# Two attentions in one kernel: A's value projection moved behind B's query and key projections, and the row maxima 52 steps ahead instead of 24

## The chip, the cores and the metric

The kernel runs on 1 core of one Trainium2 chip. A core has a matrix engine (TensorE, PE in the profile, with PEld for its weight loads), a vector engine (VectorE, DVE), an engine for activations (ScalarE, ACT), a general one (GpSimd, POOL), a queue that issues the DMAs here (SyncE, SP), and 16 DMA engines. Each engine runs its own instructions in program order. PE writes only to the accumulator memory of 8 banks (`ps_st`), from which ACT and DVE read.

The metric is the device time of one execution in microseconds (us), lower is better. Before the change it is 1758.52 us, the median of 3 runs (1756.85 to 1760.27).

## What is computed

Two attentions over the same shapes (sequence S = 2048, D = 640, 32 heads of 20 columns), each with its own x, weights and output projection; the two outputs stand side by side.

```python
def _A_ref(x, wqkv, wo):                    # sliding window: 8 keys, 2 apart
    qkv = (x @ wqkv) -> q, k, v             # (1, 32, 2048, 20) each
    idx = pos[:, None] - (arange(8) * 2)    # negative positions are masked
    logits = einsum("bhsd,bhswd->bhsw", q, k[idx]) * 20 ** -0.5
    o = einsum("bhsw,bhswd->bhsd", softmax(logits), v[idx])
    return o @ wo
def _B_ref(x, wqkv, wo):                    # full attention
    p = softmax(einsum("bhqd,bhkd->bhqk", q, k) * 20 ** -0.5)
    return einsum("bhqk,bhkd->bhqd", p, v) @ wo
return concatenate([a, b], axis=-1)
```

## The kernel before

**Precision.** Every operand x or W of a projection is split in two parts, hi and lo (`split`: a copy, then a subtraction), and a product is three passes (`PASSES`): hi·hi, hi·lo, lo·hi. With the contraction of 640 cut into `KC` = 5 chunks of 128, one output tile of a projection is 15 matmuls.

**Stage 1, projections.** First A's 1920 columns q, k, v, in `NA` = 4 column groups (`A_COLS`: 512, 384, 512 and 512 wide), each for 16 row tiles of 128 positions: 15 matmuls per tile, then a copy by ACT (`a_store`) and a store to memory. Then B's q and k, transposed: 40 groups of 15 matmuls 512 wide (the loop over `m`, `n`, `j`). Then B's v: 32 groups (`v_group`) of one row tile and half of the columns (320). From the seventh group on such a group runs in row halves: 30 matmuls with a contraction of 64, in two banks at once, which POOL adds (`ve<-ve,more`). x of A and B (`xn`, `xl`) lies in four big buffers; when B's v is computed, two of its four chunks have been overwritten by the first heads' q and k (`bq`, `bk`) and are loaded again.

**Stage 2, the loop over B's attention.** The heads go in 8 stacks of 4 (`NG`, `GH`); for each stack there are 4 blocks of queries (`NQC`) and 16 blocks of keys (`NKB`), `NS` = 512 steps in all. A step has for PE: 4 matmuls for scores (`b_qk`/`s_matmul`, contraction 62 rows, in the trace `ps_st<-bq,bk 62*128`), 4 for the row maxima of a step that comes later (`m_matmul`, 60 rows, `ps_st<-bk,bq 60*128`), and the 4 products with v (`b_pv`, `ps_st<-e,vb`; 8 records in the trace). DVE reduces the maxima (`mx<-ps_st`, 512 elements or, where two banks lie side by side, 1024 at once), ACT does the exponentials (`e<-ps_st`, 4 per step) and copies the products out (`more`), POOL adds these to `braw`. The maxima of 16 steps together make one unit; at its end (`max_rows`) they are turned by DVE, split by POOL, sent through memory (`mdr`) and enter the score matmuls as two more rows of `bq`.

The maxima of step i + `LEAD` are computed at step i. The first `LEAD` = 24 are computed ahead of the loop, one after each of the v groups (`b_max`), and in the last `LEAD` steps there are none. The order of the loop's matmuls is a string, `ORDER`: V starts a step, S is two score matmuls, M two maxima, Y one of each, N two single maxima, H a piece of A's output projection, and the digits are the banks.

**A's attention** runs on POOL beside all this: 128 units (`UNITS`), 64 of scores (`akv<-akv,aq` and a tree of additions) and 64 of values (`akv<-akv,al`, `ao`), four of each for a tile of 128 positions. Each unit's k or v rows (`akv`) are loaded two units ahead. In the loop a unit's pieces are handed out by an estimate of POOL's time, `STEP` = 2.47 us per step. In stage 1 a unit is handed out at some of B's q and k groups (`a_unit`).

## Time and profile before

The profiled execution took 1756.04 us; from its first to its last instruction (the span) it is 1754.3 us.

| what | us | from |
|---|---|---|
| time, median of 3 | 1758.52 | runs |
| time of the profiled execution | 1756.04 | its run |
| span of the profiled execution | 1754.3 | page, first line |
| busy PE / DVE / ACT / POOL | 1736.7 / 1335.1 / 1341.2 / 1253.5 | page, part 1 |
| A's projections, from the first full run of matmuls | 8.2 to 211.7 | PE's timeline |
| B's q and k | 211.7 to 348.5 | PE's timeline |
| B's v, with 24 maxima | 348.5 to 428.5 | PE's timeline |
| the 488 steps that have maxima | 428.5 to 1639.4 | PE's timeline |
| the last steps and the end of B's output projection | 1639.4 to 1754.3 | PE's timeline |

How to read it: a group of instructions is named out<-in by the tiles it writes and reads. Two numbers go with it, the time in which at least one of the group ran (busy), and the mean duration of one; where instructions of an engine overlap, the count times the mean is more than the busy time. Matmuls are pipelined, and their ends are modelled, so the distance from one start to the next says more of PE than the busy share. PEclk is the clock granted to PE, 1.00 being full.

### The profile page before, as it was taken

How to read it: one execution, taken by the hardware profiler on the slowest of the kernel's cores; microseconds unless marked ns; L12 is line 12 of the kernel's file. 1: busy time of each engine (PE TensorE's matmuls, PEld its weight loads, DVE VectorE, ACT ScalarE, POOL GpSimd, SP SyncE). 2: the span in 40 equal slices, each digit the busy share in tenths (PEclk: the TensorE clock that was granted, in tenths of full speed). 3: DMA queues.
4: the chain of work that ended last, by engine and by line, in shares of the span. 5: the costliest groups of instructions: out<-in, count | busy, mean ns of one | idle time of the engine just before them, and what ended most of it. 6: DMA issues, size and time to landing. Idle time of an engine off the chain costs nothing.

```text
span 1754.3 us, 33331 instructions
## 1 busy us (share of the span) xinstructions
PE 1736.7 (99%) x12051; PEld 1000.7 (57%) x12051; DVE 1335.1 (76%) x1792; ACT 1341.2 (76%) x2649; POOL 1253.5 (71%) x1128
## 2 busy tenths in 40 slices
PE   9999999999999999999999999999999999999999
PEld 8988888898335444444445444443444444453569
DVE  3100232368999999999999999999999989999300
ACT  4222322233999999999999999999999989999981
POOL 0000058335899999999999999999999998447242
PEclk9999999999999999999999999999999999999999
DMA  6323597763644444364435336344444534122123
GB/s 232 113 97 107 175 307 251 263 190 114 193 128 130 128 134 141 109 170 130 139 110 163 117 105 174 117 153 124 142 128 126 142 117 118 33 60 77 33 71 116
DMA packets 191197, 240.32 MB, mean 137 GB/s; under 512 B 89020, under 2 KB 115260, under 8 KB 190040
## 3 DMA queue, kind: packets, MB, share of 16 engines
q1 hardware_dynamic: 190456, 237.54, 44.4%
q8 instruction: 94, 1.54, 0.4%
q14 instruction: 71, 0.58, 0.1%
q10 hardware_dynamic: 576, 0.66, 0.1%
HBM read 173.21 MB, written 64.91 MB: 136 GB/s over the span
## 4 chain that ended last, share of the span: by engine, by line
PE 70%; POOL 11%; DVE 10%; DMA 5%; issue 2%; ACT 1%; SPq 1%; POOLq 0%; DVEq 0%; ACTq 0%
PE ps_st L66 70%; DVE mx L66 10%; POOL akv L66 6%; POOL braw L66 3%; ACT e L66 1%; SPq L66 1%; DMA bq<-qb_d 1%; DMA stg<-wo_a 1%; DMA bk<-kb_d 1%; DMA akv<-va_d 1%; POOL ao L66 1%; POOL aot L66 1%; POOL ww L66 0%; POOL al L66 0%; DMA vb_d<-ve 0%
## 5 line engine op out<-in xcount | busy, mean ns | idle before, releaser
L66 DVE TENSOR_REDUCE mx<-ps_st 128x1 f32<-128x512 f32 (+1 forms) x1470 | 1214.8, 891 | 29.4 <-PE ps_st L66 25.6
L66 ACT ACTIVATE e<-ps_st 128x512 f32<-128x512 f32 x2048 | 1069.2, 618 | 56.9 <-PE ps_st L66 38.6
L66 PE MATMUL ps_st<-bq,bk 62*128 62x512 f32 x2048 | 563.3, 437 | 7.8 <-DMA bq<-mdr 3.6
L66 PE MATMUL ps_st<-bk,bq 60*128 60x512 f32 x2048 | 551.3, 437 | 4.1 <-DVE mx L66 2.4
L66 PE MATMUL ps_st<-e,vb 128*32 128x512 f32 x4096 | 544.0, 605 | 0.7 <-ACT e L66 0.2
L66 PEld LDWEIGHTS ps_st<-bq,bk 62*128 62x128 f32 x2048 | 282.3, 184 | 416.7 <-ACT e L66 267.6
L66 POOL TENSOR_TENSOR akv<-akv,aq 128x1280 f32<-128x1280 f32 x64 | 189.0, 2953 | 234.0 <-DMA akv<-ka_d 234.0
L66 POOL TENSOR_TENSOR braw<-braw,more 128x512 f32<-128x512 f32 x224 | 288.1, 1286 | 68.2 <-ACT more L66 67.7
L66 PEld LDWEIGHTS ps_st<-bk,bq 60*128 60x128 f32 x2048 | 257.8, 184 | 108.5 <-DVE mx L66 54.0
L66 POOL TENSOR_TENSOR akv<-akv 128x640 f32<-128x640 f32 (+3 forms) x304 | 282.4, 929 | 14.3
L66 ACT COPY ro<-ps_st 128x320 f32<-128x320 f32 (+2 forms) x156 | 72.2, 491 | 175.4 <-PE ps_st L66 125.8
L66 PEld LDWEIGHTS ps_st<-e,vb 128*32 128x32 f32 x4096 | 82.2, 108 | 152.1 <-issue 75.8
L66 POOL TENSOR_TENSOR akv<-akv,al 128x1280 f32<-128x1280 f32 x64 | 152.1, 2377 | 0.2
L66 ACT COPY more<-ps_st 128x512 f32<-128x512 f32 (+1 forms) x248 | 144.7, 584 | 3.9 <-PE ps_st L66 2.4
L66 PE MATMUL ps_st<-wc,xn 128*128 128x512 f32 (+1 forms) x576 | 133.5, 376 | 0.0
L66 PE MATMUL ps_st<-ww,xn 64*128 64x320 f32 (+1 forms) x1056 | 125.1, 310 | 0.2 <-ACT ve L66 0.2
L66 PEld LDWEIGHTS ps_st<-ww,xn 64*128 64x128 f32 (+1 forms) x1056 | 116.0, 186 | 13.7 <-ACT e L66 7.1
L66 PEld LDWEIGHTS ps_st<-wc,xn 128*128 128x128 f32 x576 | 106.2, 188 | 17.9 <-ACT xn L66 0.4
L66 PE MATMUL ps_st<-xn,w 128*128 128x512 f32 x480 | 115.8, 390 | 0.0
L66 PEld LDWEIGHTS ps_st<-xn,w 128*128 128x128 f32 x480 | 90.1, 188 | 19.4
L66 ACT CAST pr<-ps_st 128x512 fp32r<-128x512 f32 x40 | 23.5, 587 | 101.5 <-PE ps_st L66 98.7
L66 PE MATMUL ps_st<-ww,aot 64*128 64x320 f32 x960 | 99.4, 308 | 0.0
(66 smaller groups left out, 1011.2 us busy)
## 6 DMA issues: line engine op xcount, KB each, us to landing
akv<-ka_d SPq DMA_DIRECT2D x128, 320.0 KB
akv<-va_d SPq DMA_DIRECT2D x128, 320.0 KB
kb_d<-pr SPq DMA_DIRECT2D x20, 512.0 KB
qb_d<-pr SPq DMA_DIRECT2D x20, 512.0 KB
bk<-kb_d SPq DMA_DIRECT2D x16, 640.0 KB
bq<-qb_d SPq DMA_DIRECT2D x64, 160.0 KB
rb<-s_d SPq DMA_DIRECT2D x128, 64.0 KB
stg<-xb SPq DMA_DIRECT2D x12, 512.0 KB
```

The costliest lines, as they stand in the source:

```text
L66: return self.tc.keep_in_program_order(op(*a, **k))
```

## The change

1. A's projections before B's are q and k only: `A_COLS` has three groups of 512, 256 and 512 columns.
2. A's v is computed after B's q and k, as B's v is: A's 32 groups of 320 columns, then B's 32. For this x of A is loaded and split a second time, chunk by chunk, and then x of B (`x_load`; the lo part by POOL for 7 of the 8 chunks, before for 2).
3. Of these 64 groups 52 run in row halves, but in another way: two groups at once, group one on the upper rows of the array and group two on the lower ones, then the other way round, so that each adds up in one bank. POOL's additions `ve<-ve,more` are gone. The first 4 groups, and 8 at the end (two of them inside the loop, as before), run plain.
4. `LEAD` is 52: after each of the 52 groups in row halves stands one `b_max`. The loop keeps its 488 steps with an `ORDER` (`TAIL` = 24 steps follow), but has 460 steps' maxima in them. `ORDER` is a new string.
5. A's units: the scores run 3 tiles ahead of the values (`R_AHEAD`), the values wait until A's v rows are there (`v_rows`), and units are handed out by POOL's estimated time in stage 1 too (`a_pace`). `STEP` is 2.4. A unit of values is not begun while two finished tiles wait to be turned.
6. The loads of the next stack's q and k start at step 1 of a stack, not 4, and the first eight go two per step.

```diff
-LEAD = 24
+LEAD = 52
+TAIL = 24
+R_AHEAD = 3
-STEP = 2.47
+STEP = 2.4
+QK_US = 3.42
+V_US = 2.72
-    A_COLS = [0, 512, 896, 1408, 3 * D]
+    A_COLS = [0, 512, 768, 2 * D]
...
+    UNITS = [(t, c) for k in range(NT + R_AHEAD) for t, cs in ((k - R_AHEAD, range(4, WIN)), (k, range(4))) if 0 <= t < NT for c in cs]
...
+            while any(u[1] >= 4 and v_rows[0] <= u[0] for u in UNITS[n:n + 3]) or c == 4 and len(done_a) > 1:
+                yield False
...
+    def a_pace(us):
+        gp.us = max(gp.us, us - 2.5)
+        while gp.us < us + AHEAD and next(a_work, 0) is not False:
+            if not a_work.gi_frame:
+                break
...
-                if 4 < groups < 34 and groups * 2 % 5 < 2:
-                    a_unit()
+                if groups > 4:
+                    a_pace(QK_US * groups)
...
+    def v_matmuls(c, half, s, p, r=None, start=True, stop=True):
+        rows = slice(0, 128) if r is None else slice(r * HALF, r * HALF + HALF)
+        for k in range(KC):
+            for i, (wi, xi) in enumerate(PASSES):
+                yield pe.matmul(p[:, :320], chunk(XV[c][0], xi, k)[rows, s % 4 * 128:s % 4 * 128 + 128], WV[c // 4][half][wi][rows, k],
+                                start=start and k == 0 and i == 0, stop=stop and k == KC - 1 and i == 2)
...
+    def v_tick(us, maxima=True):
+        for i in islice(steps, int(maxima)):
+            b_max(i)
+        tick()
...
+        v_us[0] += us
+        a_pace(v_us[0])
+    def x_load(c, w):
+        x, pieces = x_pieces((xa, xb)[c // 4], c % 4, gp)
+        XV.append((x, pieces))
+        wait[0] = w
+        for fn in pieces:
+            fn()
...
+    x_load(1, 5)
+    for block in range(15):
+        c, half = divmod(block, 2)
+        s0 = c % 4 * 4
+        if block in (0, 14):
+            for s in range(s0, s0 + 4):
+                v_group(c, half, s)
+                v_tick(2.2, False)
+        else:
+            ps4 = [bank() for _ in range(4)]
+            for second in range(2):
+                for u in range(2):
+                    for _ in zip(*(v_matmuls(c, half, s0 + 2 * u + (r ^ second), ps4[2 * u + (r ^ second)], r, second == 0, second == 1) for r in range(2))):
+                        pass
...
+                    v_tick(V_US)
+        if half:
+            if c < 6:
+                x_load(c + 2, 3)
+            if c < 4:
+                after(2, v_rows.__setitem__, 0, 4 * c + 4)
...
-        if sub == 4 and g + 1 < NG:
-            k_loads, q_loads = b_pieces(g + 1)
+        if sub == (1 if g else 2) and g + 1 < NG:
+            k_loads, q_loads = b_pieces(g + 1) if g else ([], q1_loads)
...
-                after(1 + 2 * n, fn)
+                after(1 + (n // 2 if n < 8 else 2 * n - 12), fn)
```

Where this moves instructions is shown at three places. The first is PE's program in A's projections, at the seam between the first and the second column group (`wc` and `wd` are the chunks 0 to 2 and 3 to 4 of the weight, `xn` and `xl` those of x). Before:

```order
L66 MATMUL ps_st<-wc,xn 128x512 x9
L66 MATMUL ps_st<-wd,xn 128x512 x3
L66 MATMUL ps_st<-wd,xl 128x512 x3
L66 MATMUL ps_st<-wc,xn 128x384 x9
L66 MATMUL ps_st<-wd,xn 128x384 x3
L66 MATMUL ps_st<-wd,xl 128x384 x3
```

After:

```order
L70 MATMUL ps_st<-wc,xn 128x512 x9
L70 MATMUL ps_st<-wd,xn 128x512 x3
L70 MATMUL ps_st<-wd,xl 128x512 x3
L70 MATMUL ps_st<-wc,xn 128x256 x9
L70 MATMUL ps_st<-wd,xn 128x256 x3
L70 MATMUL ps_st<-wd,xl 128x256 x3
```

The second group's 240 matmuls are 256 wide in place of 384, and one of the three groups of 512 (another 240 matmuls) is gone from this stage.

The second place is DVE's program from the end of B's q and k to the first steps of the loop (`ww` is a half of the weights of v being split, `mx` the maxima, `128x2` a reduction of 1024 elements, `128x1` one of 512; `mtr` is the turn at a unit's end). Before:

```order
L66 TENSOR_REDUCE mx4_2648<-ps_st_66 128x2 x32
L66 TENSOR_REDUCE mx1_2486<-mx4_2648 128x16
L66 STREAM_TRANSPOSE mtr_3298<-mx1_2486 128x32
L66 TENSOR_REDUCE mx4_3339<-ps_st_66 128x2 x16
L66 TENSOR_REDUCE mx4_3339<-ps_st_66 128x1
L66 TENSOR_REDUCE mx4_3339<-ps_st_66 128x2 x2
```

After, the first unit and the beginning of the second:

```order
L70 TENSOR_REDUCE mx4_2292<-ps_st_66 128x2 x12
L70 RECIPROCAL am_1543<-am_1543 128x32
L70 TENSOR_REDUCE mx4_2292<-ps_st_66 128x2 x16
L70 TENSOR_REDUCE am_2865<-al_1696 128x32
L70 TENSOR_REDUCE mx4_2292<-ps_st_66 128x2 x4
L70 TENSOR_REDUCE mx1_2156<-mx4_2292 128x16
L70 STREAM_TRANSPOSE mtr_2956<-mx1_2156 128x32
L70 TENSOR_REDUCE mx4_2994<-ps_st_66 128x2 x4
```

Before, 48 reductions of 1024 elements (24 steps) stand ahead of the loop's first single one; after the change 104 do (52 steps), with pieces of A's softmax (`am`, `al`) between them.

The third place is POOL's program in the groups of v (`ve<-ve,more` adds the row halves, `xn<-stg,xn` and `xl<-stg,xl` make the lo part of a chunk of x, `akv` and `al` are A's units). Before:

```order
L66 TENSOR_TENSOR ve<-ve,more 128x16x20 x7
L66 TENSOR_TENSOR xn<-stg,xn 128x1024 x2
L66 TENSOR_TENSOR xl<-stg,xl 128x512
L66 TENSOR_TENSOR ve<-ve,more 128x16x20 x8
L66 TENSOR_TENSOR xn<-stg,xn 128x1024 x2
```

After:

```order
L70 TENSOR_TENSOR xn<-stg,xn 128x1024 x2
L70 TENSOR_TENSOR xl<-stg,xl 128x512
L70 TENSOR_TENSOR al<-al,am 128x256
L70 TENSOR_TENSOR akv<-akv,aq 128x1280
L70 TENSOR_TENSOR akv<-akv 128x2x320
L70 TENSOR_TENSOR xn<-stg,xn 128x1024 x2
L70 TENSOR_TENSOR xl<-stg,xl 128x512
L70 TENSOR_TENSOR akv<-akv 128x2x160
```

The additions of the halves are gone, and the lo parts of x, which PE needs for the next groups, now stand in one line with A's units.

More of the change, by code (lines that the diff above doesn't have):

```diff
@@ L867, in attention_pair, with b_row @@
     steps = iter(range(LEAD))
[L868 to L871 removed]
+    WV = [[w0, w1], [None, None]]
+    def b_row(half, s, p):
         ve = ones[s % 4]
         to = ve[:, :16 * VC].rearrange("p (h c) -> p h c", c=VC)[:, :, :DH]
[L874 to L892 removed]
@@ L895, in attention_pair, with a_row @@
-    V_GROUPS = [(n, half, s) for n in (2, 3, 0, 1) for half in range(2) for s in range(4 * n, 4 * n + 4)]
-    v_late = V_GROUPS[-LAG:]
-    for n, half, s in V_GROUPS[:-LAG]:
-        v_group(n, half, s, groups > 5)
+        act.copy(to, p[:, :320].rearrange("p (h d) -> p h d", d=DH))
+        give(p)
+        c = 16 * VC + 11 * half
+        after(1, sp.dma_start, vb_d[s * 128:(s + 1) * 128, half * 16 * VC:half * 16 * VC + c], ve[:, :c])
+    def a_row(half, s, p):
+        hf, r0 = divmod(s * 128, HS)
+        store_rows(p, va_d[hf, PAD + r0:PAD + r0 + 128, half * 320:half * 320 + 320])
@@ new lines, in v_matmuls, with v_group @@
+    def v_matmuls(c, half, s, p, r=None, start=True, stop=True):
[4 more added lines that the diff above has]
+                                start=start and k == 0 and i == 0, stop=stop and k == KC - 1 and i == 2)
+    def v_group(c, half, s):
+        p = bank()
+        for _ in v_matmuls(c, half, s, p):
+            pass
+        (b_row if c > 3 else a_row)(half, s, p)
@@ L951, in begin @@
             run_jobs(soft_jobs, 1)
[L952 removed]
+        if done_a and done_a[0][0] <= 0 and len(turned) + len(turn_jobs) < 2:
             a_turn(*done_a.pop(0)[1:])
@@ L956, in begin @@
         while i >= A_FROM and gp.us < i * STEP + AHEAD:
-            if next(a_work, 0) == 0:
+            if next(a_work, 0) is False:
+                break
+            if not a_work.gi_frame:
                 for d in done_a:
@@ L1058, in attention_pair @@
     loop[1] = False
-    for i in range(NS - LEAD, NS + LAG):
+    for i in range(NS - TAIL, NS + LAG):
         begin(i)
```

219 lines of the change are left out of this document (99 added, 120 removed).

## The prediction

> **What bounds the kernel now.** I read the page first, then the busy time per stage, then per stage what DVE, ACT and PE wait for. The page:
>
> ```profile
> span 1754.3 us, 33331 instructions
> PE 1736.7 (99%) x12051; PEld 1000.7 (57%) x12051; DVE 1335.1 (76%) x1792; ACT 1341.2 (76%) x2649; POOL 1253.5 (71%) x1128
> ```
>
> PE's 99% is a share of modelled ends and hides what it waits for, so I cut the span where PE's timeline changes its work. The columns are the stretch, its length, then busy PE, PEld, DVE, ACT, POOL, the granted clock and the DMA share.
>
> ```profile
> 8.20:211.70 203.50, 203.49 (x949) 174.78 (x949) 31.83 (x43) 59.98 (x106) 0.00 (x0) 1.00 0.43 141
> 211.70:348.50 136.80, 136.80 (x602) 112.61 (x601) 45.02 (x59) 35.25 (x58) 79.19 (x68) 1.00 0.79 269
> 348.50:428.50 80.00, 79.26 (x903) 74.72 (x903) 57.15 (x52) 26.74 (x62) 30.82 (x31) 1.00 0.52 163
> 428.50:1639.40 1210.90, 1198.84 (x8794) 547.97 (x8792) 1194.25 (x1626) 1147.74 (x2281) 1105.40 (x982) 1.00 0.43 124
> 1639.40:1754.30 114.90, 111.45 (x782) 84.63 (x780) 4.76 (x10) 67.80 (x140) 34.65 (x33) 1.00 0.26 83
> ```
>
> The first three stretches are PE's: nothing else is busy for more than 0.72 of them. The fourth, the 488 steps with maxima, is DVE's: busy 1194.25 of 1210.9 us, 98.6%, where ACT has 94.8% and POOL 91.3%. Of what is DVE's time made, and what does it wait for there (428.5 to 1639.4)?
>
> ```profile
> L66 DVE TENSOR_REDUCE mx<-ps_st 128x1 f32<-128x512 f32 (+1 forms) x1425 | 1161.9, 881 | 11.8 <-PE ps_st L66 8.0
> L66 DVE TENSOR_REDUCE am<-al 128x32 f32<-128x256 f32 x14 | 8.6, 614 | 3.6 <-POOL al L66 3.6
> ```
>
> 1161.9 us are the maxima themselves. Is it really DVE and not POOL, which is as full until about 1500 us (the last of the busy times in the first pair of rows)? The exponentials (4 per step, in the second pair of rows) count the steps with POOL full and with POOL half idle:
>
> ```profile
> 428.50:1500.00 1071.50, 1060.46 (x7776) 485.33 (x7776) 1055.79 (x1435) 1014.17 (x2016) 1034.06 (x912) 1.00 0.46 134
> 1500.00:1639.40 139.40, 138.38 (x1022) 62.64 (x1024) 138.46 (x192) 133.57 (x266) 71.34 (x70) 1.00 0.19 53
> ```
>
> ```profile
> 450.00:1420.00 970.00, 420.95 (x3160) 62.29 (x3160) 825.32 (x1579) 1.00 0.46 135
> 1500.00:1620.00 120.00, 52.13 (x392) 7.64 (x392) 101.86 (x196) 1.00 0.22 61
> ```
>
> 970 / (1579 / 4) = 2.457 us per step, then 120 / (196 / 4) = 2.449. POOL's relief gives nothing, so A's units on POOL are covered now, and moving them is worth something only through what they delay.
>
> **The change part by part.**
>
> *A's projections.* PE's rows for one row tile, by the distance of the starts:
>
> ```profile
> 86.53 1.72 PE L66 MATMUL ps_st<-wc,xn 128*128 128x384 f32 x9
> ...
> 89.13 1.72 PE L66 MATMUL ps_st<-wc,xn 128*128 128x384 f32 x9
> ...
> 204.82 2.21 PE L66 MATMUL ps_st<-wc,xn 128*128 128x512 f32 x9
> ...
> 208.26 2.21 PE L66 MATMUL ps_st<-wc,xn 128*128 128x512 f32 x9
> ...
> 350.70 1.91 PE L66 MATMUL ps_st<-ww,xn 128*128 128x320 f32 x12
> ...
> 352.89 1.92 PE L66 MATMUL ps_st<-ww,xn 128*128 128x320 f32 x12
> ```
>
> 15 matmuls take 3.44 us at 512 columns, 2.60 at 384, 2.19 at 320. One group of 512 goes: 16 x 3.44 = 55.0 us. The group of 384 becomes one of 256, which the trace does not have. The three rows lie on a line (0.84 us per 128 columns), which gives 1.76 at 256, and a gain of 16 x 0.84 = 13.4; if weight loads set a floor at the 320 row, it is 16 x (2.60 - 2.19) = 6.6. I take the line, since 320 still lies on it. Sum: -68.4 (or -61.6). The weight loads of this stage:
>
> ```profile
> L66 PEld LDWEIGHTS ps_st<-wc,xn 128*128 128x128 f32 x576 | 106.2, 188 | 17.9 <-ACT xn L66 0.4
> ```
>
> They last 188 ns each, more than the line's 1.76 / 15 = 0.117 us per matmul, but overlap each other, so the row settles nothing. The Trainium skill ("TensorE: Matmul & The Clock Gate", LDWEIGHTS) puts a load of 128 columns at about 107 ns whatever the contraction, which would set no floor above the line: by the page -68.4, by the longer loads of the row -61.6. B's q and k, 136.8 us, do not change.
>
> *The groups of v.* Now 62 groups before the loop in place of 30. What one in row halves with its maximum costs:
>
> ```profile
> 417.72 0.69 PE L66 MATMUL ps_st<-bk,bq 60*128 60x512 f32 x4
> ...
> 423.64 1.92 PE L66 MATMUL ps_st<-ww,xn 64*128 64x320 f32 x24
> 425.40 0.60 PE L66 MATMUL ps_st<-ww,xl 64*128 64x320 f32 x6
> 425.84 0.63 PE L66 MATMUL ps_st<-bk,bq 60*128 60x512 f32 x4
> ...
> 428.52 0.68 PE L66 MATMUL ps_st<-bk,bq 60*128 60x512 f32 x4
> ```
>
> ```profile
> L66 DVE TENSOR_REDUCE mx<-ps_st 128x2 f32<-128x1024 f32 x578 | 696.9, 1215 | 20.6 <-PE ps_st L66 19.3
> ```
>
> Four periods in 10.80 us, 2.70 each, of which 2.20 (423.64 to 425.84) are the group: halves cost PE what a plain group does. Two groups together are 60 such matmuls where before they were two times 30, so I take the same. 52 x 2.70 + 10 x 2.19 = 162.3 us, against 80.0: **+82.3**. DVE has two reductions of 1.2 us per period (below) and is covered. POOL's additions of the halves go (hidden, worth 0).
>
> *The first maximum* comes sooner and needs q from memory:
>
> ```profile
> 348.50 1.93 PE L66 MATMUL ps_st<-ww,xn 128*128 128x320 f32 x12
> ...
> 352.57 2.87 SPq L66 DMA_DIRECT2D bq<-qb_d  x4
> ...
> 365.25 0.73 PE L66 MATMUL ps_st<-bk,bq 60*128 60x512 f32 x3 [0.54 <-DMA bq<-qb_d]
> ```
>
> The load was issued 4.1 us into the stage and had landed 16.7 us into it. After the change PE gets there after 4 plain groups and one half pair, 4 x 2.19 + 2.2 = 11.0 us. It waits up to 5.7 us; behind it in PE's queue stand all further groups, so the wait is paid in full. I take **+5**.
>
> So the loop starts -68.4 + 82.3 + 5 = **+18.9 us later**. The second load of x is 8 chunks; its issues on SP stand between the groups, its lo parts on POOL:
>
> ```profile
> L66 POOL TENSOR_TENSOR xn<-stg,xn 128x1024 fp32r<-128x1024 f32 x4 | 9.6, 2408 | 0.3
> L66 POOL TENSOR_TENSOR xl<-stg,xl 128x512 fp32r<-128x512 f32 x2 | 2.6, 1292 | 0.0
> ```
>
> One chunk is 2 x 2.41 + 1.29 = 6.1 us of POOL, handed over three groups after its load and needed five groups (13.5 us) later: hidden if POOL is less than 7.4 us behind. I count 0, its price is below.
>
> *The loop.* 28 of 488 steps' maxima leave it, 28 x 4 = 112 reductions of 512 elements. The window above holds 533 wide and 892 single ones, 1958 halves in 1161.9 us, 0.593 us each: -66.5 us of DVE. Wide reductions become a smaller share (454 of the loop, with 932 single), which gives some 4 us back. DVE's busy time falls from 1194.3 to about 1132 us. What is late next is ACT, 1147.7 us, whose work does not change. Before, the loop was 1210.9 / 1194.3 = 1.014 times its fullest engine's busy time. The same 1.4% over ACT gives 1164; over DVE, 1148, since ACT's busy time counts the overlap of exponentials with gaps between them. I take **1160 us**, 2.38 per step, nearer to ACT's. That is -50.9.
>
> Two more edits act on waits only: the scores running three tiles ahead and the larger lead give A's softmax and the turned maxima more time. The trace has one such wait of size, the 3.6 us of `am` on POOL above (it reached PE):
>
> ```profile
> 1432.13 0.79 PE L66 MATMUL ps_st<-bq,bk 62*128 62x512 f32 x1 [3.14 <-DVE mx L66]
> ...
> 1430.00:1438.00 8.00, 5.87 (x24) 2.68 (x24) 5.67 (x8) 3.12 (x6) 7.76 (x8) 0.61 0.55 179
> ```
>
> The wait was followed by a stretch with the clock at 0.61. Some 8 us hang on it; I leave them inside the 1.4%, since new waits can take its place. The Trainium skill ("TensorE: Matmul & The Clock Gate", Part 1) says that PE idle for a window of about 3.4 us gets half its clock until it was busy for as long. By that rule, with which the trace agrees here (0.61 after 3.14 us of idling), the 5 us wait at the first maximum would cost 2 to 3 us more, and the sum be some 3 us higher.
>
> The earlier loads of the next stack and the end (114.9 us, PE's) I count at 0: the next stack's q and k are hidden behind steps in either case.
>
> *Sum:* 1756.04 + 18.9 - 50.9 = 1724.0 for an execution like the profiled one. That one lies 2.5 us below the median of the runs shown, so I forecast 1726.5, rounded **1727**.
>
> **The rivals.**
>
> 1. *The step is set by the round of banks, not by DVE.* PE fills a bank, ACT empties it, PE may fill it again. For it:
>
> ```profile
> L66 PEld LDWEIGHTS ps_st<-bq,bk 62*128 62x128 f32 x2048 | 282.3, 184 | 416.7 <-ACT e L66 267.6
> ```
>
> The score matmuls' weight loads wait for ACT most of all. Against it: DVE is idle for 11.8 us before its maxima, ACT for 63 in all (1210.9 - 1147.7). If the steps stay near 2.45, fewer maxima bring nothing and the loop takes 1205: 1756 + 18.9 - 6 + 2.5 = 1771, slower. It decides from a loop above 1192 us, 2.44 per step, on. Chance 0.13.
>
> 2. *Lo parts of x late on POOL.* If POOL runs over 7.4 us behind in the groups of v, PE stands before each of 7 chunks, up to 6.1 us, 43 in all. At half of that 1748. Chance 0.08.
>
> 3. *DVE stays the limit,* ACT's overlap being free. Then 1.4% over 1132, less the 8 us around the clock's fall, about 1137: 1704. Chance 0.14.
>
> 4. *A near tie.* DVE and ACT within 2% of each other, POOL close behind: each one's short waits no longer fall into another's, and the loop takes 1180 to 1192. 1747 to 1759. Chance 0.13.
>
> That the change does not do what it says (the maxima leave the loop) is excluded by the order of the instructions.
>
> **How the numbers follow.** My forecast (loop 1148 to 1175) has 0.52. The range goes from 1698 (below rival 3, with the clock's fall gone) to 1762 (all of rivals 2 and 4), leaving out most of rival 1 and tails, together about 0.18. Faster by over 0.2%, below 1755 (about what a measurement of this kernel can tell): 0.52 + 0.14 + 0.10 of rival 4 + 0.05 of rival 2 = 0.81. Within 0.2%: 0.05. Slower: 0.14.
>
> **What would show it.** The end of A's projections near 143 us (150 if a floor exists); 2.70 us from maximum to maximum in the groups of v; PE's wait for `bq<-qb_d` before the first; the loop's start near 447; DVE in the loop near 97%, ACT near 99%; 84 exponentials per 50 us where there were 81. Wrong it would be by long PE waits for POOL `xn`, or by fewer than 82 exponentials per 50 us in the loop with DVE at 93%.

## The result, and the profile after

The changed kernel takes 1779.54 us (median of 4 runs, 1776.89 to 1781.89) against 1759.02 for the kernel before (4 runs): ratio 1.0118, 95% interval 1.0099 to 1.0136. It is slower by 1.2%; the forecast was 1727, the range ended at 1762. The page of the profiled execution (1781.89 us):

```profile
span 1780.1 us, 34705 instructions
PE 1734.6 (97%) x12711; PEld 1014.8 (57%) x12711; DVE 1358.2 (76%) x1814; ACT 1340.4 (75%) x2658; POOL 1265.4 (71%) x1119
```

PE has as much work as before in a longer span. Cut at the same places as in the prediction, with the same columns (stretch, length, busy PE, PEld, DVE, ACT, POOL, clock, DMA share):

```profile
5.20:143.90 138.70, 138.65 (x724) 118.83 (x722) 28.46 (x38) 46.94 (x84) 0.00 (x0) 1.00 0.51 164
143.90:283.20 139.30, 137.38 (x602) 112.46 (x601) 48.70 (x59) 37.96 (x61) 69.05 (x67) 1.00 0.76 259
283.20:471.60 188.40, 170.54 (x1919) 159.78 (x1917) 137.50 (x129) 47.53 (x96) 142.70 (x111) 0.95 0.64 208
471.60:1665.40 1193.80, 1173.04 (x8677) 535.55 (x8678) 1138.09 (x1579) 1138.09 (x2277) 1015.55 (x895) 0.99 0.41 117
1665.40:1780.10 114.70, 111.17 (x780) 84.38 (x778) 4.55 (x10) 67.39 (x139) 34.65 (x33) 1.00 0.27 84
```

| stretch | forecast, us | measured, us | off by |
|---|---|---|---|
| A's projections, up to | 143.3 | 143.9 | +0.6 |
| B's q and k | 136.8 | 139.3 | +2.5 |
| groups of v | 162.3 + 5 | 188.4 | +21.1 |
| the 488 steps with maxima | 1160 | 1193.8 | +33.8 |
| the rest | 114.9 | 114.7 | -0.2 |

The first and the last are right. In B's q and k PE stands 1.9 us in two waits for DVE's split of the weights (`w`), which are most of the 2.5 us there; why they are there was not looked into. In the groups of v PE is idle for 17.9 us, and the clock is at 0.95. Two waits make most of it. PE's timeline at the first:

```profile
306.98 0.76 PE L70 MATMUL ps_st<-bk,bq 60*128 60x512 f32 x1 [11.00 <-DMA bq<-qb_d]
```

SP's timeline, and the clock and the DMA share (the last three columns are clock, share, GB/s) around it:

```profile
289.73 2.22 SPq L70 DMA_DIRECT2D stg<-xa  x3
293.08 0.34 SPq L70 DMA_DIRECT2D va_d<-ro  x1
293.90 7.97 SPq L70 DMA_DIRECT2D bq<-qb_d  x4
```

```profile
271.00:283.00 12.00, 12.00 (x54) 9.81 (x54) 5.08 (x7) 5.48 (x9) 0.00 (x0) 1.00 0.98 308
283.00:295.00 12.00, 11.18 (x82) 10.34 (x82) 4.51 (x7) 4.32 (x9) 0.00 (x0) 1.00 0.94 267
295.00:307.00 12.00, 1.00 (x15) 0.77 (x11) 0.03 (x1) 2.71 (x3) 3.10 (x2) 0.65 0.73 215
```

The load of bq is issued 10.7 us into the stage (4.1 before), four issues take 8 us (2.9 before), and the DMA engines have been nearly full since 271. Around the same seam of the kernel before they were at 0.79 and 0.84:

```profile
336.00:348.00 12.00, 12.00 (x54) 9.85 (x53) 4.27 (x7) 3.37 (x6) 0.00 (x0) 1.00 0.79 255
348.00:360.00 12.00, 12.00 (x82) 11.88 (x81) 2.75 (x4) 4.01 (x8) 0.00 (x0) 1.00 0.84 265
```

The second wait, on PE, on DVE and on POOL:

```profile
387.41 0.79 PE L70 MATMUL ps_st<-bk,bq 60*128 60x512 f32 x2 [4.32 <-DVE mx L70]
```

```profile
380.24 5.98 DVE L70 TENSOR_TENSOR ww<-stg,ww 128x640 fp32r<-128x640 f32 x3
386.14 4.61 DVE L70 TENSOR_REDUCE mx<-ps_st 128x2 f32<-128x1024 f32 x4
...
398.98 1.95 DVE L70 TENSOR_TENSOR ww<-stg,ww 128x640 fp32r<-128x640 f32 x3
```

```profile
379.41 2.98 POOL L70 TENSOR_TENSOR akv<-akv,aq 128x1280 f32<-128x1280 f32 x1
382.47 4.45 POOL L70 TENSOR_TENSOR akv<-akv 128x640 f32<-128x640 f32 x4
```

The same three lo parts of a weight (first half of wv_b, then the second) take DVE 5.98 us while POOL works, and 1.95 us where POOL stands. The maxima queue behind them.

In the loop DVE and ACT are now equal (95.3% of the stretch each). DVE's longest waits there, in total, times and longest:

```profile
DVE mx L70 <- PE ps_st L70: 30.9, 64, 6.6
DVE turn L70 <- POOL ww L70: 8.9, 1, 8.9
DVE sm L70 <- DMA sm<-s_d: 4.7, 2, 3.9
DVE am L70 <- POOL al L70: 3.9, 1, 3.9
```

### The profile page after: what moved, and what is told of

Read it like the earlier page. It is cut to its first block, busy times and chain, and to the rows that moved or that the text cites. A ratio compares the mean times of both kernels' runs of the same rounds, so it can differ in the third digit from the quotient of the medians.

```text
span 1780.1 us, 34705 instructions
## 1 busy us (share of the span) xinstructions
PE 1734.6 (97%) x12711; PEld 1014.8 (57%) x12711; DVE 1358.2 (76%) x1814; ACT 1340.4 (75%) x2658; POOL 1265.4 (71%) x1119
## 5 line engine op out<-in xcount | busy, mean ns | idle before, releaser
L70 PE MATMUL ps_st<-bk,bq 60*128 60x512 f32 x2048 | 563.4, 439 | 31.1 <-DVE mx L70 19.2
L70 PE MATMUL ps_st<-bq,bk 62*128 62x512 f32 x2048 | 549.9, 433 | 0.9 <-ACT e L70 0.6
L70 PEld LDWEIGHTS ps_st<-bq,bk 62*128 62x128 f32 x2048 | 274.6, 185 | 407.8 <-ACT e L70 260.1
L70 PE MATMUL ps_st<-ww,xn 64*128 64x320 f32 (+1 forms) x1776 | 189.9, 313 | 0.8 <-DVE ww L70 0.6
L70 PEld LDWEIGHTS ps_st<-ww,xn 64*128 64x128 f32 (+1 forms) x1776 | 178.3, 190 | 16.3 <-ACT e L70 8.3
L70 ACT COPY more<-ps_st 128x512 f32<-128x512 f32 x224 | 135.7, 606 | 5.3 <-PE ps_st L70 4.6
L70 POOL TENSOR_TENSOR xn<-stg,xn 128x512 fp32r<-128x512 f32 (+1 forms) x30 | 53.8, 1805 | 81.8 <-ACT xn L70 80.5
L70 PEld LDWEIGHTS ps_st<-ww,aot 64*128 64x128 f32 x960 | 91.7, 186 | 4.9 <-issue 0.7
```

The lines of the kernel that those rows point to most:

```text
L70: return self.tc.keep_in_program_order(op(*a, **k))
```

## The experiments

From here the loop is measured from the start of the first score product to the start of the last product for a maximum, both on PE, which is 3.2 us less than the prediction's stretch before the change and 2.7 less after: 1207.7 us before, 1191.1 after, forecast 1157. The places are those of one profiled execution each; the medians are of 4 to 12 runs, and the kernel before took 1757 to 1759 us on each chip.

| kernel | median, us | ratio to before | first maximum | loop starts | loop, us |
|---|---|---|---|---|---|
| before | 1759.0 | | 364.2 | 429.0 | 1207.7 |
| changed | 1779.5 | 1.0118 (1.0099 to 1.0136) | 307.0 | 471.6 | 1191.1 |
| q_first | 1778.8 | 1.0116 (1.0098 to 1.0134) | 305.0 | 469.4 | 1190.0 |
| no_x1 | 1774.5 | 1.0096 (1.0083 to 1.0110) | 301.7 | 465.9 | 1190.4 |
| q_no_x1 | 1775.3 | 1.0089 (1.0076 to 1.0103) | 301.9 | 465.7 | 1190.6 |
| early | 1772.6 | 1.0083 (1.0070 to 1.0095) | 301.1 | 463.1 | 1188.0 |
| lo_pool | 1837.2 | 1.0443 (1.0423 to 1.0463) | 306.1 | 463.8 | 1248.9 |
| lo_same | 1781.7 | 1.0137 (1.0122 to 1.0153) | 306.4 | 474.0 | 1189.6 |
| phase_late | 1841.7 | 1.0481 (1.0460 to 1.0503) | 307.3 | 471.2 | 1247.2 |
| skip7 | 1784.9 | 1.0159 (1.0143 to 1.0174) | 305.9 | 474.1 | 1191.7 |
| turn_own | 1777.2 | 1.0107 (1.0092 to 1.0122) | 306.2 | 470.0 | 1187.0 |
| spread | 1779.6 | 1.0121 (1.0106 to 1.0136) | 305.2 | 469.7 | 1190.3 |
| soft | 1780.3 | 1.0129 (1.0115 to 1.0142) | 306.0 | 470.8 | 1190.9 |
| pool_light | 1768.9 | 1.0067 (1.0054 to 1.0079) | 309.3 | 473.4 | 1177.5 |
| light_turn | 1758.4 | 1.0000 (0.9990 to 1.0009) | 307.4 | 472.3 | 1168.0 |
| acc_turn | 1767.3 | 1.0046 (1.0033 to 1.0059) | 306.2 | 469.5 | 1177.8 |
| together | 1772.9 | 1.0083 (1.0069 to 1.0097) | 302.4 | 472.1 | 1180.6 |
| together2 | 1764.5 | 1.0034 (1.0022 to 1.0047) | 296.7 | 465.9 | 1181.0 |
| together3 | 1763.3 | 1.0028 (1.0014 to 1.0042) | 296.6 | 465.1 | 1176.6 |
| together4 | 1761.7 | 1.0016 (1.0007 to 1.0026) | 297.6 | 464.2 | 1178.4 |

**The wait for the first maximum.** `q_first`: in the last q,k group

```diff
                     k_loads.pop(0)()
+                    if (n, j) == (3, 1):
+                        for _ in range(4):
+                            q_loads.pop(0)()
```

> Stack 0's first four bq loads are issued in the last q,k group, ahead of x's second reloaded piece, and nothing else is changed. Theory (single waits set by places in the program; the rest of the change costs what was forecast): PE's 11.0 us in front of the first maximum falls under 4, the half clock after it (13.65 us, about 6.8 lost) goes, and the loop starts 12 to 17 us earlier (455 to 460 instead of 471.65); the time is about 1764 (1761 to 1768), the loop itself stays at 1191. Rival (the reload of x itself: the DMA engines are at 99% there, so whoever is put first makes the other late): the wait moves to block 2, where PE waits 6 us or more for POOL's xn, and the time falls by less than 6 us (over 1773).

The time is the rival's: the loop starts only 2.2 us earlier. Its mechanism did not come: PE's wait for bq, which still landed only at 305, is now 6.9 us; x's piece landed later, but PE waits only 0.3 us for it, far from 6. `no_x1` leaves out the load itself:

```diff
-    x_load(1, 5)
+    XV.append(XV[0])
+    wait[0] = 5
+    after(5, lambda: setattr(gp, "us", gp.us + 3 * 0.2 + 2560 * 0.00212))
```

> The second piece of A's x isn't loaded again: A's v rows of tokens 512 to 1023 are computed from the first piece (a part of the computation left out: 1.25 MB of transfer, 3 casts on ACT, 3 subtractions on POOL); A's work keeps its places. Theory (the reload's transfer fills the DMA engines and SP holds the bq loads until earlier transfers have landed): PE's wait for the first maximum falls from 11.0 to under 3 us, the half clock behind it goes, the loop starts 12 to 17 us earlier (455 to 460), the loop stays at 1187 to 1191, the time is 1763 to 1768. Rival (the engines are full of q's and k's stores and bk alone, the reload only shares in it): 6 us or more of that wait stay, the time is 1773 or more.

6.28 us of the 11.0 stay, the loop starts 5.8 us earlier: as the rival had it, the reload shares in the wait, it is not the wait. `q_no_x1` has both edits.

> q_first and no_x1 together (bq's first loads early; A's x piece 1 not loaded again, so A's v rows of tokens 512 to 1023 are computed from the first piece). Theory (bq waits for the transfers ahead of it, of which the reload is one part of several): the wait for the first maximum falls from 6.3 (no_x1) and 6.9 (q_first) to 2 to 5 us, the loop starts at 461 to 465, the time is 1770 to 1774. Rival (each alone already removed what can be removed): over 5.5 us of wait stay and the loop starts at 465 or later.

Nothing more comes of it (the rival). So `early` leaves every transfer and issues them where the engines are less busy:

```diff
-                    w0, loads = wide_pieces(wv_a[0])
+                    w0, more = wide_pieces(wv_a[0])
+                    for fn in more:
+                        fn()
...
-                if m == 8 and (n, j) == (1, 1):
-                    wait[0] = 3
+                if m == 8 and (n, j) == (1, 0):
+                    wait[0] = 4
...
-                    k_loads.pop(0)()
+                        for fn in k_loads:
+                            fn()
+                    if (n, j) == (3, 0):
+                        for _ in range(4):
+                            q_loads.pop(0)()
```

> All transfers stay; those that the stage of the v groups opens with are issued one to three groups earlier, where the DMA engines are at 27 to 60% (240 to 270 us): wv_a's first half at once, x's first piece one group earlier, bk's four loads at once, bq's first four two groups before the end. Theory (the wait for the first maximum is a jam of transfers between 271 and 305, not one transfer's place, which is why q_first gained 2 us and q_first with no_x1 no more than no_x1): the wait falls from 11.0 to under 4 us, the half clock behind it goes, the loop starts at 455 to 462, the time is 1763 to 1771. Rival (what holds bq is tied to the end of the q,k groups, a buffer or the last stores, and not to the jam): 6 us or more of the wait stay and the time is 1774 or more.

The wait for bq is gone, the loop starts 8.6 us earlier. What remains is the next transfer of the jam, wv_a's second half, on PE and ACT:

```profile
296.65 3.63 PE L70 MATMUL ps_st<-ww,xn 64*128 64x320 f32 x22 [5.12 <-ACT ww L70]
```

```profile
295.88 1.95 ACT L70 CAST ww<-stg 128x640 fp32r<-128x640 f32 x3 [8.28 <-DMA stg<-wv_a]
```

The time, 1772.6, falls between the two: the theory's wait of under 4 us became 5.1.

**DVE's lo parts, and A's places.** `lo_pool` gives them to POOL:

```diff
-        WV[1][half], pieces = wide_pieces(wv_b[half])
+        WV[1][half], pieces = wide_pieces(wv_b[half], gp, act.copy)
```

> The lo parts of wv_b (two times three subtractions) are made by POOL instead of DVE; ACT still makes the hi parts. Theory: the first three took DVE 2.84, 2.15 and 1.14 us because POOL worked beside them (0.82, 0.82 and 0.48 where POOL stood still), and maxima stood behind them; PE's gap of 4.32 us at 383 and the half clock of 6.8 us behind it go, so the loop starts 6 to 9 us earlier (about 463 to 466) and the time is about 1772 (1769 to 1775). Rival 1 (PE's gap comes from the weights' transfer or from POOL being late, not from DVE): a gap of 3 us or more stays near 380 and the time stays within 3 us of 1779. Rival 2 (POOL is the bound in this stage): POOL's 8 us more push A's scores back and show as longer waits for al in the loop; the loop gets longer by what the stage gains.

The gap at 383 goes and the loop starts 7.8 us earlier, as expected; but the loop gets 58 us longer, where rival 2 had it grow by what the stage gains. The pacing had counted POOL's extra 8 us and put A's units some three steps later. `lo_same` has the same edit with that count undone, `phase_late` has the count without the work:

```diff
+    class Unpaid:
+        def tensor_tensor(self, *a):
+            us = gp.us
+            gp.tensor_tensor(*a)
+            gp.us = us
...
-        WV[1][half], pieces = wide_pieces(wv_b[half])
+        WV[1][half], pieces = wide_pieces(wv_b[half], Unpaid(), act.copy)
```

```diff
         for fn in pieces:
             fn()
+        after(2, lambda: setattr(gp, "us", gp.us + 3 * 0.2 + 1600 * 0.00212))
```

> As lo_pool (POOL makes wv_b's lo parts, some 8 us of its time), but A's work keeps the places that it has in the program of the changed kernel, where lo_pool placed every later unit of A about three steps later. Theory of the place (the loop's order table has A's turns and output products at fixed steps, so A's work placed later misses them): lo_pool's gain in the stage stays (loop starts at 463 to 466) and the loop returns from 1249 to 1188 to 1200 us; the time is 1770 to 1782. Rival (POOL's 8 us themselves made the loop 57 us longer): the loop stays over 1230, the time over 1815.

> No work is added or moved between engines; the pacing alone counts 2 times 4 us of POOL time that isn't spent (at the two loads of wv_b), so that A's later units stand about three steps later in the program, as in lo_pool. Theory of the place (the loop's order table has A's turns and output products at fixed steps): the loop gets 30 to 60 us longer than 1191, with PE waiting for aot near steps 64, 120, 184, 248, and the time is 1810 to 1840. Rival (lo_pool lost its time to POOL's extra 8 us): the loop stays within 8 us of 1191 and the time under 1790.

The two settle it: POOL's work without the shift leaves the loop at 1189.6, the shift without any work makes it 1247.2. What happens there is to be seen on PE, A's output products in the changed kernel and in phase_late:

```profile
1430.99 0.60 PE L70 MATMUL ps_st<-ww,aot 64*128 64x320 f32 x6
1431.90 0.62 PE L70 MATMUL ps_st<-ww,aot 64*128 64x320 f32 x6
1432.59 0.61 PE L70 MATMUL ps_st<-ww,aot 64*128 64x320 f32 x6
```

```profile
1423.53 3.41 PE L70 MATMUL ps_st<-ww,aot 64*128 64x320 f32 x30 [1.95 <-DVE mx L70]
1427.72 4.18 PE L70 MATMUL ps_st<-ww,aot 64*128 64x320 f32 x30 [0.78 <-ACT ro L70]
```

The order table has six of them at a time between other work. A tile that isn't ready at its place is owed, and is then made up for at once, 30 products in a piece, with maxima and exponentials standing behind: DVE's waits for PE sum to 98.9 us in phase_late's loop, to 30.9 in the changed kernel's. lo_same lost lo_pool's gain in the stage: PE then waits 3.10 us near 395 and 3.57 near 425 for banks that ACT empties late, since ACT stands for the transfers of wv_b and of x:

```profile
398.45 1.50 PE L70 MATMUL ps_st<-ww,xn 64*128 64x320 f32 x7 [3.10 <-ACT ve L70]
```

```profile
396.19 1.88 ACT L70 CAST ww<-stg 128x640 fp32r<-128x640 f32 x3 [12.37 <-DMA stg<-wv_b]
```

What makes these transfers late was not looked into, so it isn't shown that POOL has no slack in the stage.

`skip7` leaves the lo parts on DVE and takes two maxima away behind them:

```diff
-        if block in (0, 14):
+        if block in (0, 7, 14):
...
-                v_tick(2.2, False)
+                v_tick(V_US if block == 7 else 2.2, block and s - s0 < 2)
```

> The two maxima that stand behind wv_b's first lo parts on DVE are moved from block 7 to block 14, which had none; block 7's four groups are computed over all 128 rows at once. Theory (PE's 4.32 us near 383 are DVE's 6.1 us of lo parts, stretched by POOL, with maxima queued behind them): that gap and the half clock behind it go, the loop starts 5 to 9 us earlier (463 to 467), the time is 1771 to 1775. Rival (PE's gap comes from wv_b or x being late in any case): a gap of 3 us or more stays within 10 us of 383 and the time is 1777 or more.

A miss. The gap at 383 went, and PE and DVE met the next wait 11 us later: wv_b's second half, whose transfer used to land during that gap (a late wv_b is what the rival named).

```profile
400.59 0.80 PE L70 MATMUL ps_st<-bk,bq 60*128 60x512 f32 x2 [6.63 <-DVE mx L70]
```

```profile
395.08 4.11 DVE L70 TENSOR_TENSOR ww<-stg,ww 128x640 fp32r<-128x640 f32 x3 [3.88 <-ACT ww L70]
```

**The loop.** `turn_own`, `spread` and `soft` each aim at one of DVE's waits:

```diff
-        b = sb.tile([128, KC, 128], F32, tag="stg", bufs=3, name="turn")
+        b = sb.tile([128, 1024], F32, tag="last1", bufs=2, name="turn")[:, :D].rearrange("p (k c) -> p k c", c=128)
```

> The tile into which DVE turns A's finished rows is taken from a buffer pair that is idle in the loop, and no longer from the three staging buffers that wo_a's pieces use. Theory: the two transposes at 505.3 waited 8.87 us for POOL's split of wo_a only through that shared buffer; PE's gap of 8.71 us near 498 and the half clock behind it go, the first 64 steps fall from 2.64 us towards 2.45, and the time is about 1770 (1767 to 1773). Rival (the DMA engines are over 90% busy there with the next stack, so that maxima or PV wait for bk or vb in the same place): a gap of 4 us or more stays within 10 us of it, with a DMA named, and the time is 1776 or more.

```diff
-                after(1 + (n // 2 if n < 8 else 2 * n - 12), fn)
+                after(1 + (n // 2 if n < 8 else 4 * n - 28), fn)
```

> Of the next stack's loads, those that are not needed for its first maxima (from the ninth on) are issued every fourth step instead of every second. Theory: DVE's reciprocal near 1130 stood 3.85 us on sm because s_d's store and reload were behind bq loads on SP and in the DMA queue; with those spread that gap and its half clock go, the step of that stretch falls from 2.54 to under 2.42, the time is 4 to 7 us lower (1772 to 1776). Rival (that wait is a coincidence of A's fetches, not of the earlier loads): a wait of 3 us or more for sm stays or turns up at another stack, the time is within 3 us of 1779.

In `soft` both `job(soft_jobs, 3, ...)` become `job(soft_jobs, 6, ...)`.

> DVE's maximum and reciprocal of A's softmax are placed up to six steps behind POOL's products instead of three (at the latest at A's next unit). Theory that POOL has no slack: DVE no longer waits 3.9 us for al near 1325, but the time comes back elsewhere; the total stays within 4 us of 1779. Rival (only the place of the reduction was bad): the spikes at steps 344 and 8 to 72 go without a new one, the loop falls by 5 to 10 us, the time is 1769 to 1774.

None brought what its wait was worth, and only turn_own's wait went. DVE's wait for `sm` is 2.69 us in spread (3.85 in the changed kernel), but 1.77 in q_first, which leaves the loop as it was; in soft the wait for `al` grew from 3.92 to 5.40 us. More is seen in the mean step of stretches of 8 steps, from the starts of the score products (us; the stretches left out agree to within 0.06, but for step 136, where one differs by 0.11):

```
from step   changed  q_first  turn_own  spread  pool_light  light_turn
   8          3.478    3.487     2.503   3.473       3.467       2.318
  16          2.310    2.309     2.489   2.310       2.310       2.309
  72          2.435    2.439     2.868   2.436       2.442       2.437
 160          2.293    2.293     2.293   2.291       2.293       2.293
 264          3.200    2.780     2.791   2.705       2.365       2.363
 344          3.178    3.532     3.513   3.621       2.387       2.384
```

The steps repeat to some hundredths, except at a few places. turn_own clears step 8 (7.8 us) and gets 1.4 us at 16 and 3.5 at 72 in return. What spread gains at 264 (4.0 us) and loses at 344 (3.5) is not its edit's doing: q_first shifts nearly as much between the two places (3.4 and 2.8). What repeats is when DVE's wait for POOL's `al` at 344 ends: 856.0 to 857.2 us after the loop's start in the changed kernel, q_first, soft and spread, although it lasts 3.92, 6.88, 5.40 and 8.23 us (in turn_own, 852.7 us and 6.21). The changed kernel and q_first:

```profile
1328.82 0.59 DVE L70 TENSOR_REDUCE am<-al 128x32 f32<-128x256 f32 x1 [3.92 <-POOL al L70]
1325.47 0.59 DVE L70 TENSOR_REDUCE am<-al 128x32 f32<-128x256 f32 x1 [6.88 <-POOL al L70]
```

So POOL arrives there at its own time, and what the loop gains ahead of it is waited out. `pool_light` tests that by POOL's load alone:

```diff
-            after(2, pool, raws[u], raws[u], more, ALU.add)
+            after(2, light, raws[u], more)
```

(`light` adds 64 columns and counts the full 1.28 us in the pacing.)

> POOL's additions to braw (224 of 1.28 us) are made on 64 of 512 columns, so B's sums are left incomplete; A's work keeps its places. POOL gets about 200 us lighter and nothing else changes. Theory (POOL has no slack while A's attention runs: it is at 97% there, and a single wait that is taken away comes back at the next place where another engine needs POOL; turn_own got back 4 of 8 us and 'spread' none): the waits for POOL's al and ww go, the loop falls from 1191 to 1165 to 1175 us, the time is 1755 to 1765. Rival (the waits hang on places in the program and on transfers, not on how much POOL has to do): the loop stays over 1183, the time over 1773.

264 and 344 go without a substitute (13.0 us of the 13.6 by which the loop falls), and DVE's waits for `al` and `sm` with them; step 8, which hangs on a shared buffer, stays, so the time is above the 1765 of the theory:

```profile
DVE mx L70 <- PE ps_st L70: 27.2, 63, 7.1
DVE turn L70 <- POOL ww L70: 8.7, 1, 8.7
```

`light_turn` adds turn_own:

> pool_light (POOL's additions to braw on 64 of 512 columns, so B's sums are left incomplete) and turn_own together. Theory (turn_own got back 8 us at step 8 and lost 5 of them at steps 16 and 72, because POOL, without the pause, ran late there): with POOL light all of the 8 us stay, the loop goes from 1177.5 to 1168 to 1171 us, the time to 1760 to 1763. Rival (the spike at 72 belongs to the turn itself): a spike of 0.3 us or more per step stays at 72, the loop is over 1173.

Now all of step 8's gain stays (the time is 1.6 us below the theory's range). The loop's row (the loop, with the columns as above):

```profile
472.30:1640.20 1167.90, 1164.65 (x8667) 533.23 (x8668) 1135.35 (x1574) 1134.61 (x2272) 814.52 (x893) 1.00 0.42 120
```

DVE's and ACT's work is that of the changed kernel, and the clock is at 1.00. `acc_turn` relieves POOL without leaving anything out:

```diff
+            if n == 1 and u in DVE_ADDS:
+                dve.tensor_tensor(raws[u], raws[u], acc, ALU.add)
+                after(2, lambda: setattr(gp, "us", gp.us + 0.2 + 512 * 0.00212))
+            else:
+                more = spare[n % 2][:, n // 2 % 2]
+                act.copy(more, acc)
+                after(2, pool, raws[u], raws[u], more, ALU.add)
```

> turn_own, and in ten of the 32 query blocks the second part of the accumulation is added by DVE straight from PSUM (0.69 us or so) in place of ACT's copy and POOL's 1.28 us; A's work keeps its places. Nothing is left out. Theory (POOL has no slack): POOL gets 13 us lighter by step 330, the spikes at 72, 264 and 344 shrink or go (together some 18 us in turn_own); DVE pays at most 7 us, so the loop falls from 1187 to 1172 to 1180 and the time to 1763 to 1770. Rival (DVE's added 7 us are paid in full and POOL's lateness is not what the waits hang on): 1777 or more.

As the theory had it: 9.2 us off turn_own's loop, with 12.2 us taken from POOL, 5.0 from ACT, and DVE busy for 4.5 us more.

**All of it.** `together` is early, skip7 and acc_turn.

> early, skip7 and acc_turn in one; nothing is left out. Theory (the overrun is the jam at the first maximum, the lo parts, the turn behind wo_a, and POOL without slack): loop start 450 to 458, loop 1176 to 1184 (POOL has less time before the loop, so part of the spikes may return), end 117; the time is 1746 to 1756, below the kernel before. Rival (POOL has no slack in the stage either, so that what the stage gains comes back as POOL's lateness in the loop): the loop is over 1190 and the time over 1760.

The loop was as expected (the rival's loop over 1190 did not come), but skip7's cost and wv_a's lateness ate the stage's gain, and the time is over 1760.

`together2` loads both halves of wv_a ahead of their buffers:

```diff
+                if m == 6 and (n, j) == (3, 1):
+                    raw0 = raw_pieces(wv_a[0])
+                if m == 8 and (n, j) == (0, 0):
+                    w0 = raw_tiles()
+                    raw_parts(raw0, w0)
+                if m == 8 and (n, j) == (0, 1):
+                    raw1 = raw_pieces(wv_a[1])
```

> As together, with the transfers of both halves of wv_a put where the DMA engines are idle (some 250 to 264 us; together still waited 7.1 us for the second half), wv_b's second half split one group later (its transfer had become late once the gap at 383 was gone), and twelve instead of ten additions by DVE, most of them before step 344. Nothing is left out. Theory (the overrun is a sum of such waits, each hidden behind the one ahead of it): the first maximum comes at 293 to 297, the loop starts at 448 to 456, takes 1176 to 1182, the end 117; the time is 1746 to 1757. Rival (POOL has no slack in the stage: whatever the transfers save, POOL's splits of x and A's units then end last): the loop starts at 460 or later, or the loop is over 1188, and the time is 1762 or more.

`together3` and `together4` change when wv_b's lo parts are made (the number is the count of groups behind the load, first for one half, then for the other):

```diff
-        wait[0] = 2
-        for fn in pieces:
+        for n, fn in enumerate(pieces):
+            wait[0] = (2 + n, (3, 3, 4)[n])[half]
             fn()
```

> As together2 without skip7 (which cost more than it gained: maxima between groups over 128 rows took 3.1 us a pair instead of 2.70, and wv_b's second half came late), with wv_b's first three lo parts put behind three maxima one after the other, and sixteen additions by DVE instead of twelve. Nothing is left out. Theory (a sum of single waits, over a POOL without slack): the loop starts at 455 to 460, PE's gap near 383 falls apart into gaps under 3 us without a half clock, the loop takes 1174 to 1181, the time is 1749 to 1758. Rival (POOL sets the stage's end): the loop starts at 463 or later, the time is 1761 or more.

> As together3, with wv_b's second half loaded ahead of B's x piece and its lo parts one group later, two behind one maximum and one behind the next, and thirteen additions by DVE instead of sixteen. Nothing is left out. Theory (the 5.9 us near 388 in together3 are that half's transfer and its lo parts beside POOL): the gap falls under 3 us, the loop starts at 458 to 462, takes 1173 to 1178, the time is 1754 to 1760, the same as the kernel before. Rival (another wait of the stage stands behind it): a gap of 3 us or more appears before 465, the loop starts at 463 or later.

From together2 on the first maximum came at 297 to 298 (293 to 297 expected), and the loop took 1177 to 1181 us, close to what was expected; but its start stayed at 464 to 466 where 448 to 462 were expected. Starts and times are those that the rivals of together2 and together3 had named; that POOL sets the stage's end, as they have it, is not shown. In together4 PE waits nowhere before the loop for more than 3.3 us, and the start is still 16.8 us behind the forecast's 447.4. Of these, 12.6 us are eight periods of 3.0 to 7.0 us from maximum to maximum, by what they exceed 2.70. Most of them lie where lo parts or late pieces stand between maxima, and two run at a half clock, which came with waits of 1.06 and 1.76 us:

```profile
391.06 1.14 PE L71 MATMUL ps_st<-ww,xn 64*128 64x320 f32 x12 [1.06 <-DVE ww L71]
393.97 1.44 PE L71 MATMUL ps_st<-ww,xn 64*128 64x320 f32 x8 [1.76 <-DVE ww L71]
```

```profile
393.50:400.30 6.80, 5.63 (x36) 5.05 (x38) 5.78 (x8) 0.00 (x0) 6.64 (x6) 0.50 0.02 4
```

No version that computes everything beats the kernel before; the nearest is together4 with 1.0016 (1.0007 to 1.0026) of its time.

## Why the prediction was wrong, step by step

- *A's projections, "I take the line".* Right: groups of 256 columns stand 1.78 us apart (1.76 forecast), and B's q and k start at 143.9.
- *"Halves cost PE what a plain group does", 2.70 us per period.* Right where nothing disturbs: 2.66 to 2.73 us in most periods.
- *"It waits up to 5.7 us ... I take +5", and the second load of x at 0.* This step failed. It took the landing time of before and asked only whether SP's issues and POOL's splits hide. The new transfers fill the DMA engines (0.94 to 0.98 of them from 271 to 295), so the wait was 11.0 us, and the first maximum came 23.8 us into the stage instead of 16. The half clock behind it (0.50 from 300 to 310) made the first period 5.48 us instead of 2.70, the 2 to 3 us that the prediction named for it and left out of its sum. early shows that the places of the transfers make the wait; without the reload of one piece (no_x1) it is 4.7 us shorter. The prediction's own row for B's q and k had a DMA share of 0.79, where the text says that nothing else is busy for more than 0.72.
- *Lo parts of wv_b: not in the sum at all.* wv_b is now loaded in the middle of the stage, where DVE has 0.3 us of slack per period and POOL works. From the maximum that DVE starts at 378.0 us to the one at 406.5, seven periods exceed 2.70 by 9.6 us in sum. With the 7.8 and 2.8 us at the first maximum that is 20.2 of the 21.1 us. In before the same lo parts of a weight lay ahead of the first maximum (0.82, 0.82 and 0.49 us, POOL idle):

```profile
354.17 2.17 DVE L66 TENSOR_TENSOR ww<-stg,ww 128x640 fp32r<-128x640 f32 x3 [4.17 <-ACT ww L66]
```

- *The loop, "the same 1.4%".* This step failed too. DVE's busy time was right (1132 forecast, 1135.6 measured), ACT's was less than taken (1135.5, not 1147.7). The idle share was wrong: 55.5 us instead of 28 (1160 - 1132). Of it 23.1 us hang on POOL and the shared buffer (1191.1 against light_turn's 1168.0). Behind it stands "POOL's relief gives nothing", read from mean steps of before and carried over. In the changed kernel's loop POOL has less to do in all (1014.3 us against 1105.4), but while A's attention runs it is as full as before (the last of the busy times; before, then after):

```profile
600.00:1300.00 700.00, 694.49 (x5102) 316.12 (x5098) 694.36 (x946) 668.54 (x1328) 683.14 (x604) 1.00 0.46 135
600.00:1300.00 700.00, 693.81 (x5168) 315.47 (x5161) 674.42 (x946) 678.22 (x1363) 679.89 (x598) 1.00 0.47 135
```

  pool_light refutes the sentence for the changed kernel: an undisturbed step gains nothing (2.293 at 160 in both), but the places where DVE stands for POOL go, and a mean over hundreds of steps hides those. No run relieves POOL in the kernel before.
- *The remaining 11 us* (1168.0 against 1157): DVE waits for PE in many short pieces (before, then light_turn: total, times, longest), as rival 4, the near tie, has it, at about half of the least that it gave (20 us). This is read from the traces alone; no run here changes it.

```profile
DVE mx L66 <- PE ps_st L66: 8.0, 17, 1.4
DVE mx L70 <- PE ps_st L70: 26.8, 66, 6.7
```

- *Rivals.* The first names the time best (1771), and the loop (1193.8 us) is just above its mark of 1192, but not for its cause: with POOL light and the turn in its own buffer a step takes 2.39 us (1168.0 / 488), not 2.45, with the banks as they are, so their round does not hold it at 2.45. The second (x's lo parts late) did not occur in the changed kernel. The third fell.
- *Earlier loads of the next stack, the end:* at 0, as forecast; in spread, spacing the loads out gains nothing (1779.6 us).

What stays open: how much of a wait's price in the loop is the half clock behind it, since no run separates the two; what holds the stage's end in together2 to together4; and whether an order table made for A's new places, or A's units handed out more slowly (`STEP` above 2.4), would bring the loop down with nothing left out. Neither was tried.

## What to carry to other kernels

Work that is moved into a stretch has to be charged to everything there that is nearly full (the DMA engines, POOL, a vector engine with 0.3 us to spare), not only to the queue that issues it. When one wait is to be taken away, look at the next one on the same engine before counting the gain: here five edits aimed at one wait each. Three left it in place, shorter or longer (q_first, spread, soft), skip7 removed it and gained nothing, and turn_own got 4.1 of 7.8 us; in the loop the gain stayed whole only when the engine behind the waits, POOL, got less to do. Before crediting an edit with a wait that moved, look whether the wait also moves in a run that doesn't touch that stretch, as it did here between steps 264 and 344. And where a fixed order table runs beside paced work, a shift of that work by three steps can cost more (62 us) than any wait in it.

## What was not expected of the hardware

A subtraction on DVE with both operands in SBUF took 0.82 us with POOL idle and 2.84 and 2.15 us beside POOL's products. Its end follows POOL's: DVE's first lo part ran from 380.24 to 383.08, and POOL's product beside it ended at 382.39, 0.69 us before; the second ended at 385.15, 0.68 us after the next product. The Trainium skill ("SBUF — State Buffer", Who interferes with whom) says that a DVE instruction with two SBUF inputs contends with a GpSimd one that reads SBUF, and that the later one is blocked until the other ends; the trace agrees. It also says that a reduction does not contend: DVE's maxima, from PSUM, took 1.2 us with POOL busy or idle.

In the changed kernel the half clock comes with every gap of PE over 3 us: besides the first (11.0 us), after the gaps of 4.32, 8.71, 3.90 and 3.42 us the rows read 0.53, 0.65, 0.50 and 0.50 in the 5 to 6 us behind them:

```profile
387.00:392.00 5.00, 4.25 (x26) 3.65 (x28) 3.75 (x4) 0.00 (x0) 4.76 (x6) 0.53 0.87 268
506.00:512.00 6.00, 5.01 (x26) 2.06 (x30) 5.01 (x8) 3.07 (x7) 5.92 (x5) 0.65 0.17 67
1132.00:1138.00 6.00, 5.87 (x24) 1.73 (x26) 4.11 (x8) 1.95 (x4) 6.00 (x5) 0.50 0.98 300
1330.00:1336.00 6.00, 5.40 (x23) 2.06 (x27) 3.93 (x6) 2.80 (x6) 5.92 (x5) 0.50 0.63 216
```

It doesn't take so long a gap: in turn_own the clock is halved for 3.4 us behind one of 1.39 us.

```profile
667.99 0.51 PE L70 MATMUL ps_st<-bk,bq 60*128 60x512 f32 x2 [1.39 <-DVE mx L70]
```

```profile
668.60:672.10 3.50, 3.50 (x16) 1.30 (x18) 2.24 (x4) 1.29 (x3) 3.42 (x3) 0.51 0.92 256
```
